# A chunked RWKV-7 recurrence with a GELU block: N is turned on VectorE instead of through DRAM, and the inverse leaves in four transfers

## The chip, the cores and the metric

The kernel runs on one core of a Trainium2 chip. The core has five engines with instruction streams of their own: PE (TensorE, matmuls), DVE (VectorE), ACT (ScalarE), POOL (GpSimd) and SP (SyncE, which here only issues DMAs). They share the on-chip memory SBUF; matmul results go to PSUM. The metric is the time of one execution on the device in microseconds (us), lower is better. Three runs of the kernel before took 703.46, 699.96 and 700.48 us, a median of 700.48.

## The reference

All inputs are float32. There are 4 batches x 8 heads, 768 steps and a head width of 40; the recurrence's output is brought to 3072 rows of 320 and goes through a two-layer block with an exact GELU.

```python
for t in range(S):
    y[:, :, t] = np.einsum('bhd,bhde->bhe', rt, state)
    Sa = np.einsum('bhde,bhe->bhd', state, at)
    state = state * wt[:, :, None, :] - np.einsum('bhd,bhe->bhde', Sa, bt)
    state = state + np.einsum('bhd,bhe->bhde', vt, kt)
...
x = y.transpose(0, 2, 1, 3).reshape(B * S, H * D)
h = x @ w_in                                  # 320 -> 2048
out = (0.5 * h * (1 + erf(h / sqrt(2)))) @ w_out
```

## The kernel before

**Chunks.** The 768 steps are cut into 12 chunks of C = 64, numbered 0 to 11. Within a chunk the dependence of Sa on earlier steps is a strictly triangular 64x64 system per batch and head, called N; the kernel needs the inverse of identity plus N. There are 32 such systems, and they lie in one tile of 128 partitions: flat(N) is [128, 16, 64], four quarters of 32 partitions by 16 systems by 64 columns.

**The inverse.** Only the diagonal 32x32 blocks of N are inverted column by column (BL = 32); the corner between them is filled afterwards with matmuls. There are 64 diagonal blocks, and each is inverted by two partitions, one for its even rows and one for its odd rows. So Nb holds a whole 32x32 block per partition (128 x 1024 elements) and W holds 16 rows of the result per partition. `start_inverse` (L661) clears W, sets its diagonal, loads Nb and returns the steps; `columns` does 31 pairs of POOL instructions, tmp = W x Nb (L682) and W = W + tmp (L684). `make_N` (L603) brings N into Nb's layout through DRAM: four DMAs store the diagonal blocks (L620) and two load them, the second time for the other half of the partitions (L674). `store_inverse` (L690) writes W to a DRAM scratch tile inv with two DMAs on POOL's queue, `fetch_inverse` (L699) reads it with six DMAs on SP into Tt (four) and T2 (two). `turn_corner` (L781) transposes Tt's first 32 columns on DVE into L (L783); `corner` multiplies N by L into J on PE, and `joined` finishes the corner.

**The order of the work.** The order in which each engine executes is the order of the calls in the program. Nothing reorders it. The loop over c (L1293) works on chunk c, and at the same time prepares n = c + 1 and n2 = c + 2: N of n2 is made (L1390) and its inverse computed in the second half of the turn, the inverse of n is fetched (L1381, L1392), turned into L (L1409) and used at the start of the next turn. At the end of a turn DVE executes in this order: L, then `within` (L952, the transpose of the state, which ACT copies into `turned`), then the additions L999 of the block's last products into os, then the addition L831 of X. Pieces of the GELU block are pushed between as fillers by `fill()`: each chunk has four groups of 80 matmuls into ph (L1043), and from chunk 3 on seven products po (L995, `seven`, a 2x2 scheme with seven products), with their additions on DVE.

**PSUM.** Every matmul result is taken from one pool with four buffers (`duo`, L96) that are used in turn; a new result waits until the one four before it has been read. Around a turn's end PE's order is po (two products), po (the last one), J, X, ph.

**Queues.** SP issues its DMAs in order, and each waits for the DMA eight before it to land. Near a turn's end SP's order is: xt (11 DMAs that move the block's input between partitions), b rows, k rows, the inverse's first part, N to DRAM, the rest of the inverse, Nb from DRAM, a pairs of the chunk after, k pairs, VR, out. POOL's order is: the two stores of the previous inverse, the mask of VR (L637, after ACT's copy L636), the scaling of b and k rows (L492, L498), clearing and setting W (L672, L675), then the columns.

The first chunks differ: chunk 0 is inverted with matmuls, chunks 1 to 4 (NB = 4) take some inputs in another layout, and the weights are converted while they run.

Of the kernel before, what the change touches and what calls it, by code (L numbers as in the profile page):

```python
# [10 lines left out]
FP32 = mybir.dt.float32  # L11
UINT32 = mybir.dt.uint32
ALU = mybir.AluOpType
# [6 lines left out]
def kernel(  # L20
# [58 lines left out]
    TB = G * P  # L79
    NK = -(-DM // HP)  # L80
    VC = D + C
    BW = 2 * D
    REST = HP - D

# [129 lines left out]
    def load_VR(c):  # L214
        VR = turned_in.setdefault(c, {})["VR"] = VR_ring()
        for e in range(2):
            nc.sync.dma_start(out=VR[half(e)].rearrange("p g q m d -> p (g q m) d")[:, :, :D], in_=rows_of(v, c, e))
# [52 lines left out]
                            pattern=[[1, P]], channel_multiplier=-1)  # L270
    nc.gpsimd.memset(cum_m[0:C, C:P], 0.0)

    upper = const.tile([P, C], FP32, name="upper")
    for e in range(2):
        nc.gpsimd.tensor_tensor(upper[half(e)], cum_m[half(e), half(e)], ident[half(e), half(e)], ALU.subtract)
# [140 lines left out]
    def run(steps):  # L416
        for _ in steps:
            pass
# [184 lines left out]
    def make_N(c):  # L603
        t = turned_in[c]


        if c > 1 and c % 2:
            N = work.tile([P, 4 * DM], FP32, tag="spare", name="N")[:, :2 * G * NP * C]
            N = N.rearrange("p (j g n t) -> p j g n t", j=2, g=G, n=NP)
        else:  # L610
            N = work.tile([P, 2, G, NP, C], FP32, tag="turned" if c == 1 else "N", name="N")
        t["N"] = N
        masked(flat(N), products("N_ps", t["nT"], t["aT"], True))
        if c in direct:
            return
        blk = dram.tile([2, 2, 2 * G * NP, BL, BL], FP32, tag="N", name="N")
        for j in range(2):
            for z in range(2):
                at = j * HP + z * BL
                nc.sync.dma_start(out=blk[j, z].rearrange("n s t -> s n t"),  # L620
                                  in_=flat(N)[at:at + BL, :, z * BL:(z + 1) * BL])
        blocks[c] = blk
# [38 lines left out]
    def start_inverse(c, eng, place=None):  # L661

        n = P // 2
        blk = blocks.pop(c).rearrange("j z n s t -> (j z n) s t")
        if place is None:
            Nb = work.tile([P, BL * BL], FP32, tag="Nb", name="Nb")
            W = work.tile([P, BL // 2 * BL], FP32, tag="W", name="W")
            tmp = work.tile([P, BL * BL // 7], FP32, tag="tmp", name="tmp")
        else:
            Nb, W, tmp = place  # L670
        Nb, W = (t.rearrange("p (s t) -> p s t", t=BL) for t in (Nb, W))
        eng.memset(W, 0.0)  # L672
        for par in range(2):
            nc.sync.dma_start(out=Nb[par * n:(par + 1) * n], in_=blk)  # L674
            eng.memset(W[par * n:(par + 1) * n].rearrange("p s t -> p (s t)")[:, par::BL + 2][:, :BL // 2], 1.0)  # L675
        inverses[c] = W

        def columns():
            for j in range(BL - 1):
                rows, rest = j // 2 + 1, BL - 1 - j  # L680
                t = tmp[:, :rows * rest].rearrange("p (s t) -> p s t", s=rows)
                eng.tensor_tensor(t, W[:, :rows, j:j + 1].to_broadcast([P, rows, rest]),  # L682
                                  Nb[:, j:j + 1, j + 1:].to_broadcast([P, rows, rest]), ALU.mult)
                eng.tensor_tensor(W[:, :rows, j + 1:], W[:, :rows, j + 1:], t, ALU.add)  # L684
                yield
        return columns()

    stored, fetched = {}, {}

    def store_inverse(c, engs=(nc.sync,)):  # L690
        W = inverses[c]
        n = P // 2
        inv = dram.tile([2, 2, 2 * G * NP, BL, BL], FP32, tag="inv", name="inv")
        rows = inv.rearrange("j z n (s q) t -> q (j z n) s t", q=2)
        for par in range(2):
            engs[par % len(engs)].dma_start(out=rows[par], in_=W[par * n:(par + 1) * n])
        stored[c] = inv

    def fetch_inverse(c, parts=(0, 1, 2)):  # L699
        inv = stored[c]  # L700
        if c not in fetched:
            T2 = work.tile([P, G * NP, BL], FP32, tag="T2", name="T2")
            fetched[c] = inverses[c] = Tt_ring(), T2
        Tt, T2 = fetched[c]
        for z in parts:
            for j in range(2):
                at = j * HP + z * BL
                if z < 2:
                    nc.sync.dma_start(out=flat(Tt)[at:at + BL, :, z * BL:(z + 1) * BL],
                                      in_=inv[j, z].rearrange("n s t -> s n t"))  # L710
                else:
                    nc.sync.dma_start(out=T2[j * HP:j * HP + BL],
                                      in_=inv[j, 1].rearrange("(n z) s t -> z s n t", z=2)[1])

    lo = [slice(q * HP, q * HP + BL) for q in range(2)]
    hi = [slice(q * HP + BL, (q + 1) * HP) for q in range(2)]

    NBL = 2 * G * NP
    quads = [(slice(q * BL, (q + 1) * BL), slice(q % 2 * BL, (q % 2 + 1) * BL)) for q in range(4)]
    lo = [slice(q * HP, q * HP + BL) for q in range(2)]  # L720
    hi = [slice(q * HP + BL, (q + 1) * HP) for q in range(2)]
# [571 lines left out]
    for c in range(2, NCH):  # L1293
        n, n2, n3 = c + 1, c + 2, c + 3
        more, more2, more3 = n < NCH, n2 < NCH, n3 < NCH
        corner(c)
        make_X(c)
        if c > 2:
            turn_blocks(range(4, 16))
        if c == NS + 1:  # L1300
            weight_sums(3)
        if c == 2:

            seconds(1, (14, 14), last=True)
            fill()
            turn_b(n)
            make_N(n)
            run(start_inverse(n, nc.gpsimd))
            store_inverse(n, (nc.gpsimd,))
            load_r(n)  # L1310
            load_v(n)
            load_next(n2)
        else:
            fill()
        joined(c)
        if c == 2:
            pieces.reverse()
            seconds(2, last=True)
            fill()
            make_sa(c)  # L1320
            make_saT(c)
            turn_r(n)
            scale_k(n, nc.vector)
            fill()
            pieces.reverse()
            fill(2)
            turn_k(n)
            load_r(n2)
            turn_a(n2)
            fetch_pairs(n2, "b_turned", b, nc.sync, False, paired["a"])  # L1330
        else:
            if more2:
                turn_a(n2)
            if more:
                turn_k(n)
            if more2:
                load_r(n2)
                load_w(n2)
                fetch_pairs(n2, "b_turned", b, nc.sync, False, paired["a"])
            if c == 3:  # L1340
                scale_b(n)
                scale_k(n, nc.vector)
            fill()
            make_saT(c)
            sa_blocks(c, range(12))
        fill()
        if c > 2:
            sa_blocks(c, range(12, 16))
        make_y2(c)
        make_M(c)  # L1350
        if more:
            turn_v(n)
            if more2:
                load_v(n2)
        if more and c > 2:
            scale_kT(n)
            if more2:
                turn_r(n2)
        fill()
        if more2:  # L1360
            logs(n2)
        make_QY(c)
        outputs(c)
        if more2 and c == 2:
            turn_r(n2)
            fetch_pairs(n2, "k_turned", k, nc.sync, False, paired["r"])
        elif more2:
            load_kb(n2)
        pieces.append(mlp(c))
        fill()  # L1370
        if c == NS:
            weight_sums(0)
            weight_sums(1)
        if more:
            make_A(n)
        if more2:
            sums(n2)
        if c > NS:
            fill()
        if more:  # L1380
            fetch_inverse(n, (0,))  # L1381
            make_av(n)
        if more2:
            scale_a(n2)
            turn_b(n2)
        fill()
        if c == NS:
            weight_sums(2)
        if more2:
            make_N(n2)  # L1390
        if more:
            fetch_inverse(n, (1, 2))  # L1392
            make_RV(n)
        if more2:
            if c > 2:
                scale_b(n2, nc.gpsimd)
                scale_k(n2, nc.gpsimd)
            steps = start_inverse(n2, nc.gpsimd)
            if more3:
                load_a(n3)  # L1400
            if c == 2:
                load_kb(n2)
            else:
                fetch_pairs(n2, "k_turned", k, nc.sync, False, paired["r"])
            load_VR(n2)
            run(steps)
            store_inverse(n2, (nc.gpsimd,))
        if more:
            turn_corner(n)  # L1409
            turn_within()  # L1410
            turn_blocks(range(4))
        fill()
        fill()
# [31 lines left out]
```

## Time and profile before

The profile is one execution, taken with the profiler. Its span runs from the core's first to its last instruction.

| | |
|---|---|
| median of three runs | 700.48 us |
| the profiled execution | 705.17 us |
| its span | 703.5 us |
| mean granted PE clock | 0.949 of full speed |
| busy: PE, PE weight loads | 653.3 us (93%), 565.1 us (80%) |
| busy: DVE, POOL, ACT | 395.9, 382.0, 286.2 us (56%, 54%, 41%) |
| DMA | 74.64 MB in 287,935 packets |
| Nb loads and N stores, all chunks | 22 x 256 KB, 44 x 64 KB |

How to read it: "busy" counts the time in which an engine executed something. In the lines by group, the text is line, engine, operation, out<-in, shapes and how often; after the bar the busy time in us and the mean in ns of one; after the second bar the engine's idle time just before them in us, and what ended it. In a timeline a line starts with the start and the duration in us, several instructions merged into one line have an xcount, and the idle time before and who ended it stand in brackets. A window's line has its length, the busy time of PE, PE weight loads, DVE, ACT and POOL, the granted clock, the mean busy share of the DMA engines and GB/s. Idle time of an engine that nobody waits for costs nothing.

### The profile page before, as it was taken

What the parts mean: (1) busy time and instruction counts of PE and PEld (TensorE: products, weight loads), DVE (VectorE), ACT (ScalarE), POOL (GpSimd) and SP (SyncE); (2) the same over time, 40 slices, a digit from 0 to 9 for tenths busy, and PEclk for the clock granted to TensorE, in tenths of its full rate; (3) what the DMA queues carried; (4) which work ended last, traced back from release to release, by engine and by line L of the source; (5) the groups of instructions that cost most, each with busy time, mean ns of one, the idle gap of its engine ahead of it and who ended that gap; (6) DMA issues with size and microseconds to landing.
All of it is one profiled execution on the core that took longest, in us unless ns stands there. A gap on an engine that the chain in (4) does not pass through costs nothing.

```text
span 703.5 us, 35528 instructions
## 1 busy us (share of the span) xinstructions
PE 653.3 (93%) x16050; PEld 565.1 (80%) x16050; DVE 395.9 (56%) x548; ACT 286.2 (41%) x523; POOL 382.0 (54%) x812
## 2 busy tenths in 40 slices
PE   7578897879999999999999999999999989989997
PEld 4567787657777876898988998997898878969977
DVE  2334879985254683674784674864755735522403
ACT  5124674444142543444444436526425434133020
POOL 5275448820761875855846855865847847810000
PEclk9885798978999999999999999999999999989999
DMA  9589537753757749548648558567567563020100
GB/s 132 111 168 153 113 87 198 140 113 83 133 110 126 125 94 159 104 86 152 126 91 151 112 89 151 110 104 145 99 114 141 92 124 67 21 55 3 35 7 20
DMA packets 287935, 74.64 MB, mean 106 GB/s; under 512 B 265736, under 2 KB 284456, under 8 KB 287784
## 3 DMA queue, kind: packets, MB, share of 16 engines
q1 hardware_dynamic: 283360, 68.20, 53.4%
q0 software_dynamic: 864, 2.36, 2.1%
q8 instruction: 126, 2.06, 1.3%
q10 hardware_dynamic: 3560, 1.80, 0.9%
q14 instruction: 25, 0.20, 0.1%
HBM read 58.69 MB, written 9.70 MB: 97 GB/s over the span
## 4 chain that ended last, share of the span: by engine, by line
PE 70%; DVE 6%; POOL 4%; issue 4%; DMA 3%; SPq 1%; ACT 0%; DVEq 0%; POOLq 0%
PE ph L1043 27%; PE po L995 16%; PE po L1059 7%; PE QY L110 6%; POOL tmp L682 2%; POOL W L684 2%; PE J L110 2%; PE X L110 2%; PE av L110 2%; PE N_ps L110 1%; PE RV_ps L110 1%; PE saT_ps L110 1%; PE M_ps L110 1%; PE wT_ps L110 1%; PE A_ps L110 1%
## 5 line engine op out<-in xcount | busy, mean ns | idle before, releaser
L1043 PE MATMUL ph<-xt,w_in_sb 64*64 64x256 f32 x3840 | 224.8, 382 | 4.7 <-issue 4.6
L1043 PEld LDWEIGHTS ph<-xt,w_in_sb 64*64 64x64 f32 x3840 | 172.1, 135 | 39.8 <-issue 10.4
L682 POOL TENSOR_TENSOR tmp<-W,Nb 128x126 f32<-128x126 f32 (+22 forms) x310 | 130.2, 420 | 102.5 <-DMA Nb<-N 79.0
L684 POOL TENSOR_TENSOR W<-W,tmp 128x126 f32<-128x126 f32 (+22 forms) x310 | 130.3, 420 | 24.3
L1045 ACT ACTIVATE gt<-ph 128x1024 f32<-128x1024 f32 x48 | 49.1, 1023 | 108.0 <-PE ph L1043 107.8
L995 PE MATMUL po<-w_out_sb,gt 128*128 128x160 f32 x576 | 84.7, 303 | 0.0
L995 PEld LDWEIGHTS po<-w_out_sb,gt 128*128 128x128 f32 x576 | 78.9, 190 | 4.9 <-issue 3.3
L963 ACT COPY turned<-within 32x256 f32<-32x256 f32 (+3 forms) x144 | 46.4, 322 | 60.4 <-DVE within L952 58.7
L1059 PE MATMUL po<-w_out_sb,gt 128*128 128x320 f32 x192 | 56.3, 451 | 0.0
L1059 PEld LDWEIGHTS po<-w_out_sb,gt 128*128 128x128 f32 x192 | 37.1, 197 | 15.7 <-issue 2.0
L637 POOL TENSOR_TENSOR VR<-VR,upper 128x1024 f32<-128x1024 f32 x8 | 18.9, 2363 | 41.0 <-ACT VR L636 41.0
L916 DVE TENSOR_TENSOR xt<-QY,wpT 128x512 f32<-128x512 f32 x24 | 15.5, 686 | 33.0 <-PE QY L110 32.1
L872 DVE COPY SM<-sa 32x256 f32<-32x256 f32 x72 | 33.0, 458 | 1.2
L814 DVE COPY Tt<-J 32x512 f32<-32x512 f32 x9 | 6.2, 689 | 46.5 <-PE J L110 46.5
L783 DVE STREAM_TRANSPOSE L<-Tt 128x512 f32<-128x512 f32 x11 | 7.8, 711 | 43.1 <-DMA Tt<-inv 43.1
L320 ACT ACTIVATE conv<-conv,rebias 128x320 uint32<-128x320 uint32 (+1 forms) x26 | 16.1, 623 | 30.0 <-DVE conv L319 23.2
L995 PE MATMUL po<-extra,half 128*128 128x160 f32 x176 | 26.1, 303 | 0.0
L995 PEld LDWEIGHTS po<-extra,half 128*128 128x128 f32 x176 | 24.2, 190 | 0.3
L866 DVE STREAM_TRANSPOSE sa<-saT 128x1024 f32<-128x1024 f32 x9 | 11.2, 1242 | 22.3 <-ACT saT L856 22.3
L872 ACT COPY SM<-sa 32x64 f32<-32x64 f32 x72 | 17.4, 242 | 13.3 <-DVE sa L866 12.3
L1049 DVE TENSOR_TENSOR half<-gt 128x1024 f32<-128x1024 f32 x9 | 11.9, 1322 | 18.3 <-ACT gt L1045 18.3
L580 DVE TENSOR_TENSOR N<-N_ps,upper 128x1024 f32<-128x1024 f32 x12 | 14.6, 1221 | 12.3 <-PE N_ps L110 12.3
(233 smaller groups left out, 1169.3 us busy)
## 6 DMA issues: line engine op xcount, KB each, us to landing
Nb<-N SPq DMA_DIRECT2D x20, 256.0 KB
VR<-in_v_dram SPq DMA_DIRECT2D x24, 160.0 KB
out_dram<-os SPq DMA_DIRECT2D x48, 80.0 KB
b_rows<-in_b_dram SPq DMA_DIRECT2D x22, 160.0 KB
k_rows<-in_k_dram SPq DMA_DIRECT2D x22, 160.0 KB
N<-N SPq DMA_DIRECT2D x44, 64.0 KB
Tt<-inv SPq DMA_DIRECT2D x44, 64.0 KB
a_pairs<-in_a_dram SPq DMA_DIRECT2D x18, 144.0 KB
```

The source lines that it names most:

```text
L110: nc.tensor.matmul(o, lhsT, rhs, start=first, stop=True, skip_group_check=True)
L320: nc.scalar.activation(power, power, ACT.Relu, bias=rebias, scale=8.0)
L637: nc.gpsimd.tensor_tensor(to, to, upper.unsqueeze(1).to_broadcast([P, 2 * G * NP, C]), ALU.mult)
L682: eng.tensor_tensor(t, W[:, :rows, j:j + 1].to_broadcast([P, rows, rest]), Nb[:, j:j + 1, j + 1:].to_broadcast([P, rows, rest]), ALU.mult)
L684: eng.tensor_tensor(W[:, :rows, j + 1:], W[:, :rows, j + 1:], t, ALU.add)
L872: copy(t["SM"][to:to + BL, g].rearrange("p q m c -> p (q m) c")[:, :, d * BL:end], t["sa"][at:at + BL, :, to:to + end - d * BL])
L916: nc.vector.tensor_tensor(xt[:, :NP, g * P:(g + 1) * P].rearrange("p i (e t) -> p i e t", e=2), Y, wp[:, g, :, :, :C], ALU.mult)
L963: nc.scalar.copy(tn[to:to + deep, :, at:at + wide], within[0][at:at + deep, :, to:to + wide])
L995: nc.tensor.matmul(po[:, n, :DM // 2], l_[:, f], r_[:, f], start=f == 0, stop=f == NF // 2 - 1)
L1043: nc.tensor.matmul(ph[to:end, x, s], w_in_sb[half(x), kt, p * P + to:p * P + end], xt[half(x), kt], start=kt == 0, stop=kt == NK - 1)
L1045: nc.scalar.activation(gt[:, 4 * q:4 * q + 4].rearrange("p (x s) t -> p x s t", x=2), ph, ACT.Gelu)
L1059: nc.tensor.matmul(po[:, g], gt[:, f, g * P:(g + 1) * P], w_out_sb[:, f], start=f == 0, stop=f == NF - 1)
```

## The change

For chunks 5 to 11 (c > NB) N no longer goes through DRAM. Three DVE transposes write Nb directly: one over all 128 partitions and columns 0 to 31 of N, then one each over the second and the fourth quarter and columns 32 to 63, which overwrite what the first wrote there. A transpose works on 32x32 blocks: for each column t of a block it takes 32 partitions (rows) by 32 elements (16 systems, read twice) and writes one partition for each of these elements. So the partitions of W and Nb are in another order than before: quarter, parity, system. W's diagonal is set with two POOL copies from a new tile `odd`, which marks a partition's parity and is made once from the identity. The inverse leaves in four DMAs, a quarter each, in the order 0, 2, 1, 3, and the scratch tile's layout changes with it. The transposes stand between L and `within` on DVE, so `turn_corner` moves ahead of the columns and the stores in the program, and its own place on DVE's stream stays. SP loses the four stores of N and the two loads of Nb in each of these chunks.

```diff
@@ make_N
-        if c in direct:
+        if c in direct or c > NB:
             return
@@ start_inverse
         eng.memset(W, 0.0)
-        for par in range(2):
+        for y in range(2 if c > NB else 0):
+            eng.tensor_copy(W.rearrange("p s t -> p (s t)")[:, y::BL + 2][:, :BL // 2],
+                            odd[:, y:y + 1].to_broadcast([P, BL // 2]))
+        blk = None if c > NB else blocks.pop(c).rearrange("j z n s t -> (j z n) s t")
+        for par in range(0 if c > NB else 2):
             nc.sync.dma_start(out=Nb[par * n:(par + 1) * n], in_=blk)
             eng.memset(W[par * n:(par + 1) * n].rearrange("p s t -> p (s t)")[:, par::BL + 2][:, :BL // 2], 1.0)
         inverses[c] = W
+        turned_in[c]["Nb"] = Nb
@@ new
+    def turn_N(c):
+        N, Nb = flat(turned_in[c]["N"]), turned_in[c]["Nb"]
+        for q in (None, 1, 3):
+            part = slice(0, P) if q is None else slice(q * BL, (q + 1) * BL)
+            cols = slice(0, BL) if q is None else slice(BL, C)
+            nc.vector.transpose(Nb[part].rearrange("p s t -> p t s"),
+                                N[part, :, cols].rearrange("p n t -> p t n").unsqueeze(2).to_broadcast(
+                                    [part.stop - part.start, BL, 2, NBL]))
@@ store_inverse
+        if c > NB:
+            inv = stored[c] = dram.tile([4, BL, NBL, BL], FP32, tag="inv", name="inv")
+            for i, q in enumerate((0, 2, 1, 3)):
+                engs[i % len(engs)].dma_start(out=inv[q].rearrange("(s y) n t -> (y n) s t", y=2),
+                                              in_=W[q * BL:(q + 1) * BL])
+            return
@@ fetch_inverse
-                                      in_=inv[j, z].rearrange("n s t -> s n t"))
+                                      in_=inv[2 * j + z] if c > NB else inv[j, z].rearrange("n s t -> s n t"))
@@ the loop
+        if c == 2:
+            nc.vector.tensor_reduce(out=odd, in_=ident.rearrange("p (q y n) -> p y q n", q=4, y=2), op=ALU.add,
+                                    axis=mybir.AxisListType.XY)
...
+        if more:
+            turn_corner(n)
+            if c > 2 and more2:
+                turn_N(n2)
+        if more2:
             run(steps)
             store_inverse(n2, (nc.gpsimd,))
         if more:
-            turn_corner(n)
             turn_within()
             turn_blocks(range(4))
```

More of the change, by code (lines that the diff above doesn't have):

```diff
@@ L81 @@
     VC = D + C
+    NBL = 2 * G * NP
     BW = 2 * D
@@ L271 @@
     nc.gpsimd.memset(cum_m[0:C, C:P], 0.0)
+    odd = const.tile([P, 2], FP32, name="odd")
     upper = const.tile([P, C], FP32, name="upper")
@@ L663, in start_inverse @@
         n = P // 2
-        blk = blocks.pop(c).rearrange("j z n s t -> (j z n) s t")
         if place is None:
@@ L709, in fetch_inverse @@
                     nc.sync.dma_start(out=flat(Tt)[at:at + BL, :, z * BL:(z + 1) * BL],
-                                      in_=inv[j, z].rearrange("n s t -> s n t"))
+                                      in_=inv[2 * j + z] if c > NB else inv[j, z].rearrange("n s t -> s n t"))
                 else:
                     nc.sync.dma_start(out=T2[j * HP:j * HP + BL],
-                                      in_=inv[j, 1].rearrange("(n z) s t -> z s n t", z=2)[1])
+                                      in_=(inv[2 * j + 1].rearrange("s (n z) t -> z s n t", z=2) if c > NB else
+                                           inv[j, 1].rearrange("(n z) s t -> z s n t", z=2))[1])
     lo = [slice(q * HP, q * HP + BL) for q in range(2)]
     hi = [slice(q * HP + BL, (q + 1) * HP) for q in range(2)]
-    NBL = 2 * G * NP
     quads = [(slice(q * BL, (q + 1) * BL), slice(q % 2 * BL, (q % 2 + 1) * BL)) for q in range(4)]
```

## The prediction

> **What bounds the kernel now.** I read four views in this order: the page's shares, who waited for whom on PE, the timelines of DVE, SP and PE around one chunk boundary, and the granted clock in small windows. PE is the bound: 653.3 of 703.5 us busy, and from 226 us to 622.7 us 384.6 of 396.7. So a stall elsewhere counts only where PE stands still, and a delay anywhere counts once it reaches PE. The obvious stall is POOL's:
>
> ```profile
> L682 POOL TENSOR_TENSOR tmp<-W,Nb 128x126 f32<-128x126 f32 (+22 forms) x310 | 130.2, 420 | 102.5 <-DMA Nb<-N 79.0
> ```
>
> POOL stood 79.0 us waiting for Nb, but that is not PE's time. PE's own waits are these (total, times, longest):
>
> ```profile
> PE J L110 <- DVE L L783: 8.4, 4, 4.2
> ...
> PE ph L1043 <- issue: 4.6, 5, 1.5
> ```
>
> L is the first thing that the fetched inverse gives. Of the 8.4 us, 4.2 belong to chunk 2, which the change leaves alone. The rest is 0.15 us at chunk 9, 1.84 at chunk 10 and 1.87 at chunk 11: POOL's inverse runs a little slower than PE's chunk (its stores start at 259.4 us for chunk 4 and 614.2 for chunk 11, 50.7 us a chunk, against 49.5 between PE's X products), and only the last chunks feel it.
>
> Each of the two long waits costs a second time. Windows (us; busy PE, PEld, DVE, ACT, POOL; granted clock; DMA):
>
> ```profile
> 571.43:574.85 3.42, 1.58 (x118) 1.42 (x118) 2.25 (x4) 0.41 (x2) 1.88 (x4) 1.00 0.74 117
> 574.85:578.26 3.41, 3.41 (x56) 2.21 (x52) 1.73 (x5) 3.29 (x9) 0.00 (x0) 0.50 0.45 69
> ...
> 277.90:281.31 3.41, 1.96 (x39) 1.06 (x28) 1.94 (x2) 2.51 (x10) 2.94 (x7) 1.00 1.39 175
> ```
>
> With 1.84 us idle in the first window the clock of the next is halved; 1.45 us idle near 280 us halves nothing. The PE timeline has the price:
>
> ```profile
> 573.42 0.74 PE L110 MATMUL J<-L,N 32*32 32x32 f32 x64 [1.84 <-DVE L L783]
> 574.09 1.36 PE L110 MATMUL X<-st,aT 40*64 40x40 f32 x64
> 575.37 5.95 PE L1043 MATMUL ph<-xt,w_in_sb 64*64 64x256 f32 x80
> ```
>
> The same ph group takes 4.55 us undisturbed (524.75 us) and X 1.14: 1.40 + 0.22 = 1.62 us lost here, and at chunk 11 (ph 7.03, X 1.95) 2.48 + 0.81 = 3.29.
>
> **What sits behind L on DVE.** At chunk 6's boundary (start, us):
>
> ```profile
> 372.39 0.71 DVE L783 STREAM_TRANSPOSE L<-Tt 128x512 f32<-128x512 f32 x1 [3.61 <-DMA Tt<-inv]
> 373.03 1.20 DVE L952 STREAM_TRANSPOSE within<-st 128x1024 f32<-128x1024 f32 x1
> 374.15 0.28 DVE L999 TENSOR_TENSOR os<-os,po 128x160 f32<-128x160 f32 x1
> 374.47 0.58 DVE L999 TENSOR_TENSOR os<-os 128x160 f32<-128x160 f32 x1
> 375.09 0.32 DVE L999 TENSOR_TENSOR os<-os,po 128x160 f32<-128x160 f32 x1
> ```
>
> The third L999 is the last reader of a po buffer, and the psum pool has four buffers: po, po, J, X are the four before ph, so ph can't start until that add has emptied the first. PE meanwhile:
>
> ```profile
> 375.00 0.75 PE L110 MATMUL J<-L,N 32*32 32x32 f32 x64
> 375.69 1.14 PE L110 MATMUL X<-st,aT 40*64 40x40 f32 x64
> 376.64 0.64 PE L1043 MATMUL ph<-xt,w_in_sb 64*64 64x256 f32 x8
> ```
>
> The add ends at 375.41 and ph starts at 376.64: 1.2 us of slack. At chunk 9 it is spent (the add ends at 524.69, ph starts at 524.75). The change puts its work into this slack.
>
> **The change, part by part.**
>
> *N and Nb no longer go through DRAM (chunks 5 to 11).* SP loses six issues a chunk: at this boundary N took 3.41 us (x4) and Nb 1.12 (x2). POOL then waits for the DVE copy. Its own preparation ends at 375.67 (J's start + 0.7 us), and it started its columns at 380.55. Starting them 4 us earlier each chunk stops the drift, so the waits at chunks 9 to 11 go: 3.86 us of idle and 4.91 us of half clock, **minus 8.8 us**. What is late next is not the inverse: its columns take 31.9 us (582.02 to 613.9), a store lands 3.8 us after its issue, and together they end well inside 49 us.
>
> *When L comes then.* It can't come much before where the early chunks have it. SP issues xt after PE's QY, then b and k rows, then the fetch of the inverse (367.64 at this boundary, though the inverse had landed at 363.49), and the fetch lands behind the rows. L started 2.97 us before J at chunk 5 and 2.61 before at chunk 6: I take 2.8.
>
> *Three transposes on DVE between L and within.* Each covers 1024 elements a partition, also the two on 32 partitions. Nearest rows:
>
> ```profile
> L952 DVE STREAM_TRANSPOSE within<-st 128x1024 f32<-128x1024 f32 x9 | 10.8, 1203 | 0.0
> L186 DVE STREAM_TRANSPOSE nT<-a_pairs 128x1024 f32<-128x1024 f32 x8 | 9.9, 1239 | 0.0
> ...
> L783 DVE STREAM_TRANSPOSE L<-Tt 128x512 f32<-128x512 f32 x11 | 7.8, 711 | 43.1 <-DMA Tt<-inv 43.1
> ```
>
> No row reads or writes with steps as long as these (256 bytes in, 128 out); L186 writes every second element and pays nothing for it. Below, 1.2 us each; above, twice the cost per element. From 512 to 1024 elements costs 0.49 us more, so 1024 at double cost are 1.20 + 0.98 = 2.2 us. I take L186's end, 1.2 us, 3.6 for three. The add then ends at L + 2.9 (3.02 here, 2.76 at chunk 7) + 3.6 = L + 6.5 = J + 3.7, and ph, due at J + 1.64, waits 2.1 us. Six boundaries have both (chunks 5 to 10; at chunk 4 the buffer that ph takes over was emptied by ACT): **plus 12.4 us**. About half of such stalls fall with 1.7 us or more into one 3.41 us window; at (1.62 + 3.29) / 2 = 2.45 us each, 6 x 0.5 x 2.45: **plus 7.4 us** (bounds 0 and 14.7).
>
> [...]
>
> *Behind them.* within, the ACT copies into turned, and the add into avs move by 3.6 us. turned is read by QY at 392.90, 17 us after ph; avs by saT at 387.59: covered. *Four stores instead of two* cost POOL 2 x 0.83 us; L needs only the first two. POOL had 41.0 us of waits ahead of L637, 5 us a chunk, to hide it; without that cover it would still be 1.7 us on an engine that isn't the bound. *Two copies of odd* replace two memsets (0.28 us a pair; between 0 and 0.2 us more, going by L684's 0.23 for 128x16): hidden by the same waits. *odd itself*: one reduction in chunk 2's stage, under 0.5 us by L783's row, while DVE has room. DMA traffic falls by 768 KB a chunk; I count nothing for it. The 4.6 us of PE "issue" gaps I leave (bounds minus 4.6 and 0).
>
> Sum: 12.4 + 7.4 - 8.8 = plus 11.0 us. The profiled execution took 705.17 us (span 703.5), so 716.2 on its own scale; on the median of 700.48, **711.5 us**. The profiled one is 4.7 us above the median, so perhaps only 4.1 of the 8.8 are there to win.
>
> **Rivals.**
> 1. *The long steps cost double.* Three transposes take 6.6 us, ph waits 2.1 + 3.0 = 5.1 at six boundaries and each stall fills a window: 12.4 + 17.7 + 14.7 - 8.8 = plus 36.0, **736.5 us**. For it: no row has such steps. Against: L186 pays nothing at its short one. Chance 0.28.
> 2. *The stalls cost no clock.* Plus 12.4 - 8.8 = 3.6, 704.1; if PE reads ahead while it stands and the issue gaps go, down to 699.5; say **702 us**, no change. Against: 1.84 and 1.87 us both halved the clock. Chance 0.15. [...]
> 3. *Faster: L comes early enough.* With 4 us less to issue, SP reaches the fetch sooner. It decides at L = J - 4.9: from there on the add ends before ph is due and only the gain is left, **691.7 us** (696.4 if 4.1 is all there is). For it: chunk 4 had 5.5 us. Against: at chunks 5 and 6 SP was on time and L came at 2.8. Chance 0.15. That the change doesn't do what it says (Nb still late) would leave 700.5 and is within rival 2's chance.
>
> **Numbers.** Forecast 0.42, rivals 0.28, 0.15, 0.15. A measurement can tell about 0.5% from no change: faster 0.15, same 0.15, slower 0.70. The forecast's own range is 702 to 719; leaving out rival 3 and the top of rival 1 gives 699 to 740.
>
> **What would show it.** No wait for DMA Nb<-N at POOL; J never waiting for L from chunk 5 on; ph waiting for L999 at six boundaries, 2 us each, with half-clock windows behind some; Nb rows at 1.2 us. Wrong if L starts 5 us before J, if the transposes cost 2.2 us, or if ph waits without loss of clock.

## The result and the profile after

The changed kernel took **728.8 us** (median of 6 runs, 724.37 to 734.19); the kernel before took 701.21 us on the same chip (median of 6, 699.94 to 704.45). The ratio is 1.0383, 95% interval 1.0341 to 1.0424: slower, as forecast, but by 27.6 us instead of 11. The profiled execution of the changed kernel took 734.19 us with a span of 732.5, 29.0 more than before's 703.5; its mean granted clock is 0.925. Ratios and intervals leave out the few executions that were over 1.5% slower than the fastest of their kernel; medians and ranges hold all.

The waits of the change are where the prediction looked for them. The view of who waited for whom (total, times, longest), PE of the kernel after:

```profile
PE ph L1065 <- DVE os L1021: 26.1, 6, 5.1
...
PE J L111 <- DVE L L805: 4.0, 1, 4.0
```

J's one wait left is chunk 2's, so L is never late from chunk 5 on. In exchange ph waits at all six boundaries where it was expected to, but for 4.35 us each (3.82, 4.28, 3.65, 4.98, 5.12, 4.28), where the forecast had 2.1. POOL of the same kernel:

```profile
POOL tmp L688 <- DMA Nb<-N: 42.7, 2, 26.4
POOL tmp L688 <- DVE Nb L700: 25.0, 7, 5.1
```

The two waits for the DMA belong to chunks 3 and 4, which the change leaves alone. For chunks 5 to 11 POOL now waits for DVE, seven times, 25.0 us in all, where in the kernel before its seven waits for the DMA were 37.8 us (79.0 in all, less 26.0, 14.2 and 0.9 at chunks 2 to 4).

The cause of the size stands in two rows. Groups by line with shapes kept apart, DVE of the kernel after:

```profile
L700 DVE STREAM_TRANSPOSE Nb<-N 32x1024 f32<-32x1024 f32 x14 | 29.6, 2112 | 0.3
L700 DVE STREAM_TRANSPOSE Nb<-N 128x1024 f32<-128x1024 f32 x7 | 14.9, 2136 | 0.0
```

A new transpose takes 2.1 us where 1.2 was taken, on 32 partitions as on 128. At chunk 6's boundary (timeline, DVE then PE, kernel after):

```profile
380.10 0.71 DVE L805 STREAM_TRANSPOSE L<-Tt 128x512 f32<-128x512 f32 x1 [2.99 <-DMA Tt<-inv]
380.74 6.39 DVE L700 STREAM_TRANSPOSE Nb<-N 128x1024 f32<-128x1024 f32 x3
387.17 1.25 DVE L974 STREAM_TRANSPOSE within<-st 128x1024 f32<-128x1024 f32 x1
...
389.06 0.32 DVE L1021 TENSOR_TENSOR os<-os,po 128x160 f32<-128x160 f32 x1
```

```profile
383.33 0.75 PE L111 MATMUL J<-L,N 32*32 32x32 f32 x64
384.01 1.14 PE L111 MATMUL X<-st,aT 40*64 40x40 f32 x64
389.44 7.09 PE L1065 MATMUL ph<-xt,w_in_sb 64*64 64x256 f32 x80 [4.28 <-DVE os L1021]
```

The third addition ends at 389.38 us and ph starts 0.06 us later; at the other five boundaries it starts 0.05 to 0.06 us behind that addition too. This is the chain of the prediction, link by link, with a longer link in it. At chunk 4's boundary, which the prediction had excepted, the transposes run until 282.52 us and ph starts at 280.52 without a wait. And ph itself takes 7.09 us instead of 4.55. Windows (length; busy PE, PEld, DVE, ACT, POOL; clock; DMA; GB/s) of the same stretch:

```profile
385.00:388.40 3.40, 0.15 (x12) 0.04 (x4) 3.36 (x4) 0.00 (x0) 0.88 (x4) 0.91 0.94 136
388.40:391.80 3.40, 2.36 (x24) 1.47 (x28) 2.20 (x7) 3.23 (x9) 2.74 (x9) 0.50 0.63 125
391.80:395.20 3.40, 3.40 (x44) 2.00 (x40) 0.00 (x0) 2.29 (x9) 2.80 (x8) 0.58 0.22 53
```

A stretch in which PE works 0.15 us is followed by 6.83 us at half clock (387.81 to 394.63). All six stalls have such a tail, so half the clock is granted for 41.0 us of the span from 300 us on (10.2 before).

**The stretch that is compared below.** The change works between the start of J at chunk 5 and at chunk 11, on PE's timeline. That stretch took 297.15 us before (324.81 to 621.96) and 325.22 after (328.67 to 653.89): 28.1 of the span's 29.0 us. Outside it, after's start-up was 3.86 us longer (already by chunk 2, ahead of the change), and its end 2.9 shorter: before, J of chunk 11 was late, and X and ph behind it ran at half clock (1.95 and 7.03 us instead of 1.14 and 4.55).

### The profile page after: what moved, and what is told of

Read it like the earlier page. It is cut to its first block, busy times and chain, and to the rows that moved or that the text cites. A ratio compares the mean times of both kernels' runs of the same rounds, so it can differ in the third digit from the quotient of the medians.

```text
span 732.5 us, 35548 instructions
## 1 busy us (share of the span) xinstructions
PE 665.1 (91%) x16050; PEld 567.9 (78%) x16050; DVE 435.6 (59%) x570; ACT 286.1 (39%) x523; POOL 376.3 (51%) x826
## 4 chain that ended last, share of the span: by engine, by line
PE 46%; DVE 13%; SPq 10%; POOL 9%; DMA 6%; issue 4%; ACT 1%; ACTq 0%; DVEq 0%; POOLq 0%
PE ph L1065 23%; PE po L1017 11%; DVE Nb L700 6%; PE QY L111 4%; POOL tmp L688 4%; POOL W L690 4%; DMA Tt<-inv 3%; SPq L179 3%; SPq L949 2%; DMA inv<-W 1%; SPq L182 1%; DVE within L974 1%; PE po L1081 1%; PE saT_ps L111 1%; PE M_ps L111 1%
## 5 line engine op out<-in xcount | busy, mean ns | idle before, releaser
L1065 PE MATMUL ph<-xt,w_in_sb 64*64 64x256 f32 x3840 | 235.0, 396 | 27.1 <-DVE os L1021 26.1
L688 POOL TENSOR_TENSOR tmp<-W,Nb 128x126 f32<-128x126 f32 (+22 forms) x310 | 123.3, 398 | 91.3 <-DMA Nb<-N 42.7
L690 POOL TENSOR_TENSOR W<-W,tmp 128x126 f32<-128x126 f32 (+22 forms) x310 | 123.6, 399 | 24.3
L700 DVE STREAM_TRANSPOSE Nb<-N 32x1024 f32<-32x1024 f32 (+1 forms) x21 | 44.5, 2120 | 0.3
L894 DVE COPY SM<-sa 32x256 f32<-32x256 f32 x72 | 31.1, 432 | 1.2
L1017 PE MATMUL po<-extra,half 128*128 128x160 f32 x176 | 26.1, 303 | 0.0
```

What stands on the lines that cost most here:

```text
L700: nc.vector.transpose(Nb[part].rearrange("p s t -> p t s"), N[part, :, cols].rearrange("p n t -> p t n").unsqueeze(2).to_broadcast([part.s ...
L894: copy(t["SM"][to:to + BL, g].rearrange("p q m c -> p (q m) c")[:, :, d * BL:end], t["sa"][at:at + BL, :, to:to + end - d * BL])
L1017: nc.tensor.matmul(po[:, n, :DM // 2], l_[:, f], r_[:, f], start=f == 0, stop=f == NF // 2 - 1)
L1065: nc.tensor.matmul(ph[to:end, x, s], w_in_sb[half(x), kt, p * P + to:p * P + end], xt[half(x), kt], start=kt == 0, stop=kt == NK - 1)
```

## The experiments

The theory after the result: everything is the 6.39 us of DVE work ahead of the third addition, and that is the long steps' price. Its rivals: the place among the additions does not matter and something else of the change (the four stores, POOL's new wait) holds PE up; or the transposes are dear for another reason than their steps. Experiments 1 to 3 and 5 take the length or the place away, 4 splits the steps, 6 asks whether the path matters at all, and 7 looks for a version that is faster. The edits are shown shortened. The kernel before is timed beside each, with medians from 699.69 to 701.34.

**1. The transposes behind the additions.**

```diff
-            turn_N(n2)
-            run(steps); store_inverse(n2, (nc.gpsimd,))
             turn_within(); turn_blocks(range(4)); fill(); fill()
+            turn_N(n2)
+            run(steps); store_inverse(n2, (nc.gpsimd,))
```

> The same three transposes, but behind the additions L1021 instead of in front of within. Order theory (what costs is that ph on TensorE waits for additions queued behind the transposes): ph no longer waits for L1021 at the six boundaries (26.1 us in the changed kernel goes to under 2), no half-clock window behind them, time 692 to 700 us, below the kernel before. Work theory (6.4 us more of VectorE and the new layouts cost wherever they stand, since the later transposes of a, k and sa come later too): the loss moves to other waits and the time stays at 715 or more. What could spoil it for the order theory: POOL's columns start some 8 us behind J instead of 4.2, so that the next inverse comes only about when L wants it.

Measured: 706.91 us (704.09 to 709.87), ratio 1.0103 (1.0034 to 1.0172), between what the two theories had said. The waits of ph are gone (0.46 us at most), so the place of the transposes made them. But the gain didn't come, since another wait took their place. PE's waits in this kernel:

```profile
PE J L111 <- DVE L L805: 13.3, 8, 4.3
```

4.3 of it is chunk 2's; 8.7 us fall on chunks 5 to 11. POOL's columns now start 9.2 us behind J (333.27, J at 324.10; in the kernel before it was 4.3 there, 329.08), and the inverse, which takes the rest of the turn, comes late at six of seven boundaries instead of at the last three. The clause of the expectation that told what could spoil it is what happened. So N must be turned early enough for POOL as well as late enough for PE.

**2. Short steps, and only one transpose.** Two kernels with the transposes in the change's place, first all three with contiguous input and output, then the first one alone:

```diff
-            nc.vector.transpose(Nb[part].rearrange("p s t -> p t s"), N[part, :, cols]...)
+            nc.vector.transpose(Nb[part].rearrange("p s t -> p (s t)"),
+                                N[part].rearrange("p n t -> p (n t)"))
```

> The transposes at their place and of their size, but with input and output contiguous, so that what lands in Nb is another order of the values (the result is not the reference's). Step theory (the 2.1 us of a transpose are the long steps): 1.2 us each, 3.6 together, as the forecast took it; ph then waits about 1.3 to 2.1 us at six boundaries, 8 to 13 us in all instead of 26.1, and the time is 703 to 715 us. If a transpose stays at 2.1 us, it is not the steps but the place or the size, and the time stays near 729.

```diff
-        for q in (None, 1, 3):
+        for q in (None,):
```

> Only the first of the three transposes (2.1 us) is made; the second and fourth quarter of Nb then hold the wrong columns. Order theory: the third addition ends at about J + 2.1 (L at J - 2.9, plus 2.9, plus 2.1), ph is due at J + 1.64, so it waits 0.3 to 1 us at a boundary, too short to lower the clock: 695 to 701 us. Together with the memset (1 us), three short ones (3.6) and three long ones (6.4) it gives the wait as a function of what stands in front of the additions; the work theory has the time in proportion to VectorE's work: 6.4 us cost 28, so 2.1 us would cost about 9, 710 us.

Measured: 701.83 us (697.39 to 710.44) with short steps, ratio 1.0018 (0.9977 to 1.006); 696.15 us (694.12 to 698.32) with one transpose, ratio 0.9945 (0.9917 to 0.9973). Without the long steps each element is also read once, not twice. The short steps' groups and PE's wait:

```profile
L700 DVE STREAM_TRANSPOSE Nb<-N 32x1024 f32<-32x1024 f32 x14 | 17.3, 1238 | 0.3
L700 DVE STREAM_TRANSPOSE Nb<-N 128x1024 f32<-128x1024 f32 x7 | 8.4, 1202 | 0.0
```

```profile
PE ph L1064 <- DVE os L1020: 4.1, 4, 1.4
```

Same instructions, same number of elements, same place, 1.20 to 1.24 us: the steps are the price. Even at this price, the one that the prediction took, the stalls sum to 4.1 us and not 12.4, since L starts 5.4, 5.5, 3.9, 3.7, 4.2 and 3.4 us ahead of J, where 2.8 was taken. With one transpose (2.14 us) they sum to 0.66.

**3. No transpose at all.** Nb is cleared by one DVE memset.

```diff
-        for q in (None, 1, 3):
-            ...
+        nc.vector.memset(turned_in[c]["Nb"], 0.0)
```

> The three transposes are left out; one contiguous memset of Nb on VectorE, about 1 us, stands in their place, so that the inverse is that of the identity. Order theory: the slack of about 1.2 us between the third addition and ph takes it, ph waits for next to nothing, J never waits for L, and what is left is the gain alone: 8.8 us by the profile of before, 692 to 697 us. If instead the new path itself (four transfers, copies of odd, another layout in DRAM) costs, the time stays above 700.

Measured: 696.6 us (693.35 to 698.91), ratio 0.994 (0.9905 to 0.9975). No wait of ph, none of J from chunk 5 on. So what the change has to give without its cost is about 4.2 us of the time (0.6%), not 8.8. Between the two profiled executions it is more: the stretch from chunk 5 to 11 took 290.51 us, 6.6 less than before, and what follows it 77.9 instead of 81.5.

**4. Long steps on one side only.** Input steps of 256 bytes and contiguous output, then contiguous input and output steps of 128 bytes.

```diff
-            nc.vector.transpose(Nb[part].rearrange("p s t -> p t s"),
+            nc.vector.transpose(Nb[part].rearrange("p s t -> p (s t)"),
```

> Only the input keeps its long steps (256 bytes from element to element); the output is contiguous, so Nb holds another order of the values. If the reading side makes the transposes cost 2.12 us instead of 1.23, they stay at 2.1 us and the time near 729; if the writing side does, they fall to 1.2 and the time to about 702, that of the short steps. If each side adds a part, something between.

```diff
-                                N[part, :, cols].rearrange("p n t -> p t n").unsqueeze(2)...
+                                N[part].rearrange("p n (x t) -> p (n x) t", x=2))
```

> The counterpart: the input is contiguous, only the output keeps its steps of 128 bytes; Nb holds other values. 2.1 us and about 729 if writing is the dear side or if either is enough, 1.2 us and about 702 if reading is.

Measured, one run each: 718.7 and 718.84 us beside 700.19. Long input, then long output:

```profile
L700 DVE STREAM_TRANSPOSE Nb<-N 128x1024 f32<-128x1024 f32 x7 | 13.6, 1946 | 0.0
```

```profile
L700 DVE STREAM_TRANSPOSE Nb<-N 128x1024 f32<-128x1024 f32 x7 | 13.7, 1960 | 0.0
```

Neither expectation was right: it isn't one side that pays. Either side alone brings 1.95 us (some 0.7 more than with short steps), both together 2.12. The long output alone reads each element once, so the double reading is not needed for the price; on the input side it was not tried without the long steps. ph waited 16.6 and 17.1 us at the six boundaries.

**5. The same instructions spread out.** One transpose ahead of L, one between L and within, one behind the additions.

```diff
+                turn_N(n2, (None,))
             turn_corner(n)
-                turn_N(n2)
+                turn_N(n2, (1,))
-            run(steps); store_inverse(n2, (nc.gpsimd,))
             turn_within(); turn_blocks(range(4)); fill(); fill()
+                turn_N(n2, (3,))
+            run(steps); store_inverse(n2, (nc.gpsimd,))
```

> All three transposes, spread: the first in front of L, where VectorE stood idle for 2 to 5 us, the second between L and within, the third behind the additions. Order theory: in front of the additions only one is left beside what the idle time takes, as in the kernel with one transpose, so ph waits under 1 us a boundary; Nb is ready at about J + 4, 4 us sooner than with all three behind the additions, so the next inverse is in time and J doesn't wait for L: 693 to 699 us. If the sum of VectorE's work counts instead, it stays near the 707 of the kernel with all three behind the additions.

Measured: 693.65 us (691.1 to 697.29), ratio 0.9924 (0.9889 to 0.9959). All three transposes are there and as dear as ever (2.15 to 2.18 us); ph waits 0.12 us at most, J not at all, and POOL starts its columns 4.1 to 5.1 us behind J at chunks 5 to 10, where the kernel before went from 4.3 to 8.6. DVE's total work alone costs PE nothing.

**6. The kernel before with the transposes added.** N and Nb still go through DRAM; the three transposes write a tile that nobody reads.

```diff
             turn_corner(n)
+            if c > 2 and more2:
+                idle_turns(n2)
             turn_within()
```

> The kernel before, with N and Nb through DRAM as ever, and the three long-step transposes of N added between L and within; they write a tile that nobody reads. Order theory: ph waits for the third addition at the six boundaries, 4 to 5 us each, with half-clock windows behind, as in the changed kernel. What the forecast's sum makes of it: the changed kernel's 728.8 plus the gain that is not taken here (4.7 us by the memset kernel), 733. What speaks for less: with 55 us a chunk instead of 49, POOL's loop (50.7 us) is no longer the slower one, so the waits for L at the last chunks go here too, and it comes out at the changed kernel's 729 or a little under: then gain and loss never were a sum. Work or path theory (the new path costs): it stays near 701 to 705.

Measured: 725.52 us (725.02 to 726.19) beside 699.69, ratio 1.0353 (1.0309 to 1.0396). PE's waits:

```profile
PE ph L1054 <- DVE os L1010: 27.9, 6, 5.2
...
PE J L110 <- DVE L L794: 3.4, 2, 3.0
```

The loss is there without the change's path (the intervals of the two ratios overlap). The case that the expectation named against the forecast's sum is what happened: the late L of the last chunks is gone here too, although Nb still comes through DRAM. The stretch from chunk 5 to 11 took 323.48 us, against 325.22 in the changed kernel. PE's chunk had become 53.9 us long, more than the 50.7 that POOL took for one, so the inverse no longer fell behind. On top of the stalls the new path brings nothing: they had already bought what it was to bring.

**7. Gathered first, turned once.** ACT copies the four quarters of N side by side into a tile Nd, and one transpose turns it.

```diff
+    def gather_N(c):
+        ...
+        for rows, cols in quads:
+            nc.scalar.copy(Nd[rows], N[rows, :, cols])
...
-        for q in (None, 1, 3):
-            ...
+        nc.vector.transpose(Nb.rearrange("p s t -> p t s"),
+                            Nd.rearrange("p n t -> p t n").unsqueeze(2).to_broadcast([P, BL, 2, NBL]))
...
+            gather_N(n2)
             turn_corner(n)
```

> ScalarE first copies the four quarters' diagonal columns side by side (4 copies of 32x512, about 0.57 us each, in its idle time behind the copy of VR), so that one transpose over 128 partitions does what took three; it stands between L and within. Order theory: one long-step transpose of 2.1 us, the same wait of ph as the kernel with one transpose (0.7 us in all), 694 to 698 us, with all of Nb in place. What could spoil it: the copies end late (N is masked at J - 6, they need 2.3 us, so J - 3), or delay ScalarE's copies into turned.

> The kernel with ScalarE's gather and one transpose once more, with more rounds, since its first four runs spread from 689.3 to 698.6. It beats the kernel before if the order theory is right: 692 to 697 us, ratio 0.987 to 0.994.

Measured: 692.32 us (689.27 to 698.6), ratio 0.9869 (0.9796 to 0.9943), and in the second run with more rounds 692.05 us (690.1 to 693.8), ratio 0.9865 (0.9827 to 0.9903): the lowest median of all kernels here, 7.6 us under the kernel before; experiment 5's interval overlaps with it. DVE, then ACT, at chunk 6's boundary of the second run:

```profile
368.85 0.71 DVE L809 STREAM_TRANSPOSE L<-Tt 128x512 f32<-128x512 f32 x1 [2.83 <-DMA Tt<-inv]
369.49 2.10 DVE L705 STREAM_TRANSPOSE Nb<-Nd 128x1024 f32<-128x1024 f32 x1
371.69 1.25 DVE L978 STREAM_TRANSPOSE within<-st 128x1024 f32<-128x1024 f32 x1
...
373.53 0.32 DVE L1025 TENSOR_TENSOR os<-os,po 128x160 f32<-128x160 f32 x1
```

```profile
365.67 1.01 ACT L638 COPY VR<-RV_ps 128x1024 f32<-128x1024 f32 x1 [1.77 <-PE RV_ps L111]
366.57 2.49 ACT L700 COPY Nd<-N 32x512 f32<-32x512 f32 x4
372.97 1.65 ACT L989 COPY turned<-within 32x256 f32<-32x256 f32 x4 [3.90 <-DVE within L978]
```

The one transpose still has its long steps (2.10 us), but the third addition ends at 373.85, when ph is just due (373.91). The four copies fill a hole of ACT's: behind them it still waits 3.90 us for within. In the stretch from chunk 5 to 11 the two runs took 290.75 and 291.08 us, 6 less than the kernel before but no less than with the memset (290.51) or one transpose (288.93). Their profiled executions, of one and the same kernel, reach J of chunk 5 at 328.28 and 322.54 us, so the lead over those two, some 4 us by the medians, does not show in the stretch, and what it comes from is open.

## Why the prediction came out as it did

| work on DVE ahead of the third addition | its length, us | ph's waits, us | J of chunk 5 to J of chunk 11, us | time, us |
|---|---|---|---|---|
| nothing (kernel before) | 0 | 0.1 | 297.15 | about 700 |
| one memset (3) | 0.91 | 0 | 290.51 | 696.6 |
| one transpose, long steps (2) | 2.14 | 0.66 | 288.93 | 696.15 |
| three, short steps (2) | 3.68 | 4.1 | 293.80 | 701.83 |
| three, long on one side (4) | 5.85 | 16.6, 17.1 | 312.62, 314.56 | 718.7, 718.84 |
| three, long on both, old path (6) | 6.35 | 27.9 | 323.48 | 725.52 |
| three, long on both (the change) | 6.36 | 26.1 | 325.22 | 728.8 |

The length is 3 x the transposes' mean where the kernel has three. The waits and the time grow slowly until the slack in front of ph is spent, and steeply from there.

**The bound and the chain: right.** The time is lost on PE, at ph, through the third addition and the buffer of the PSUM pool, at chunks 5 to 10; from J of chunk 5 to J of chunk 11 PE has no other idle time above 0.15 us. Experiment 1 removes that wait by the place, experiment 6 makes it with the three transposes alone.

**The step that failed is "I take L186's end, 1.2 us, 3.6 for three".** The three took 6.39 at chunk 6. No row before had such steps, and of the two bounds (1.2 and 2.2) the dear one, whose doubling was the author's estimate, was right to 4%: rival 1's mechanism with its price. At chunk 6 the wait follows by the prediction's own sum: ph is due at J + 1.64, L came 3.23 us ahead of J, and the third addition ended 9.28 us behind L (2.9 + 6.39): 9.28 - 3.23 - 1.64 = 4.4, measured 4.28. The waits grew from the forecast 12.4 to 26.1 us. With short steps the same transposes took 1.20 to 1.24 us (experiment 2), with the long ones 2.12.

**"About half of such stalls" was the second failure.** 2.45 us for a stall that drops the clock was right: the six ph groups behind them took 7.34, 7.09, 7.41, 7.05, 6.81 and 6.88 us, 2.55 more than 4.55 on average. But it was all six, 15.3 us instead of 7.4: each stall was longer than 3.41 us (3.65 to 5.12), and two windows of 3.41 us at half clock followed each. (In the profiles before and after, every stretch of one granted clock lasts a whole number of 3.41 us, but for the last, which is cut off.) The 1.7 us in one window that the forecast counted with are a figure that no run shows: one stall of 1.60 us (experiment 4) was followed by half clock, of two of 1.66 us (experiment 1) one was.

**The gain of 8.8 us came true in the sum, but not through the new path.** The waits for L at the last chunks and the half clock behind them are gone in the changed kernel: 3.86 us of waits and 1.62 at chunk 10 in the stretch, and most of the 2.9 by which its end is shorter. But experiment 6 keeps the old path and loses them too, since their cause, POOL's 50.7 us against PE's 49.5, ends as soon as PE slows down. What the path has to give alone is experiment 3's: 4.2 us on the time, near the 4.1 that the prediction had named as the other possibility. (Of the 8.4 us in the prediction's view of J's waits, the fourth wait is chunk 1's 0.43, not chunk 9's 0.15; the 3.86 us hold without it.)

So the sum, on the stretch: the waits and half clock, 26.1 + 15.3 = 41.4 us, explain more than the 28.1 measured. From J's start to the second ph group of a turn PE took 7.85 us before and 13.89 after (mean of the six boundaries), 36.2 in all; of the difference of 5.2 to 41.4, 4.2 stood in that place before as gaps (1.54, 0.80, 0.28) and half clock at chunk 10 (1.62), which were not the change's. The rest of the turn fell from 41.68 to 40.31 us, 8.2 in all. 3.9 of that are J's old waits. Another 3.0 are idle times of PE for which the profile shows no cause: 2.6 us ahead of QY at five of the six turns and 0.5 at a later ph before, 0.1 after. PE of the kernel before:

```profile
PE QY L110 <- issue: 2.6, 5, 0.7
```

In experiment 6 they are gone too (0.16 us), so it isn't the new path that took them away. The remaining 1.3 us weren't settled.

**L at J - 2.8 was half right.** In the changed kernel it was 3.2 on average, but where PE isn't held up it comes earlier (experiment 2), which is rival 3's condition come true in part. With the price it assumed, the forecast of 711.5 us would have been some 10 us too slow: experiment 2 took 701.83. That the time lay inside the wide range of 699 to 740 us, outside the forecast's own 702 to 719, owes something to errors of opposite sign: waits and half clock were 21.6 us above the forecast, and elsewhere the turns got 13.3 us shorter (41.4 - 28.1), where 8.8 were counted, 3.3 of them behind the stretch.

**Rival 1** said 736.5 us: its mechanism and its price were right, and it was 7.7 us too high: its stalls of 5.1 us were 4.35, 4.0 us less in all, its 14.7 us of half clock were 15.3, and where it took 8.8 us off, 13.3 came off in the stretch. **Rival 2** fell: the stalls cost clock every time, 2.55 us each on average. What was costed at nothing stayed at nothing as far as the runs show: the four stores took POOL 0.65 us each, the two copies of odd 0.34 us a pair, and POOL waited 25.0 us for Nb, so they were covered. The four stores weren't tried without the rest, so what they bring or cost is open; so are the "issue" gaps of PE, which were 1.0 us at ph in the changed kernel and 6.2 in the fastest one, and whether PE reads ahead while it stands, which no run shows.

## What to carry to other kernels

Put work on an engine's queue where nothing that the bound engine waits for stands behind it, and count the slack from the reader of the PSUM buffer that is next to be reused, not from the transfer you want to hide; the same three instructions cost 4% in one place and nothing when spread around it. An access pattern without a row in the profile is to be priced at its dear bound until it has been measured, because a stall grows by the whole overrun once the slack is spent, and each stall here cost over half of its length again in clock (2.55 us behind 4.35). Waits that come from one engine's loop being longer than another's go away when that other loop gets longer, whatever made it longer, so such a gain says nothing for a change that also slows the other loop.

## What the runs showed of the hardware

- **The cost of steps in a DVE transpose isn't a sum of its sides.** 128x1024 float32: 1.20 us with contiguous sides, 1.95 with 256-byte input steps (each element read twice, as in the change), 1.96 with 128-byte output steps, 2.14 with both. And 32 partitions cost what 128 do (2.11 and 2.14 us).
- **How much idle time halves PE's clock.** Stalls of 3.5 to 5.2 us (the changed kernel and experiments 4 and 6) were followed by 6.83 us at half clock each time. Of the seven from 2.9 to 3.4 us in experiment 4, four had 6.83 us and three 3.41; the two of 1.60 and 1.72 us in the long-input kernel had 3.41 each, and the one of 1.52 us in the long-output kernel none. A stall of 1.66 us in experiment 1 had 3.41 us at chunk 6 and none at chunk 8; in the kernel before, the one of 1.84 us had 3.41 and the one of 1.87 had 6.83. So it isn't the length of a stall alone that decides: of these seven from 1.52 to 1.87 us, five had half clock behind them.
- **Tails at even distance.** In the changed kernel the half-clock stretches begin at 333.2, 387.8, 442.4, 497.0, 551.6 and 606.3 us, 54.6 us apart, which is 16 windows of 3.41 (in experiment 6 they are 54.6 us apart too), while J to J varied from 54.0 to 55.3 between chunks 5 and 10. Whether the clock's windows set the turn's length there was not tried.
